# Attention in a recurrent-memory layer: scores turned keys-by-queries, row sums by a product with ones, division by exp(-ln(sum)), and filling work placed elsewhere

## The chip, the cores and the metric

The kernel runs on one core of one Trainium2 chip. The metric is the device time of one execution in microseconds (us). A run is one execution, and the medians below are of three or more runs. In the text PE is TensorE (the matrix engine), ACT is ScalarE, DVE is VectorE and POOL is GpSimd.

## The reference

The model alternates two kinds of layer, A, B, A, B, each on the normalized stream and each added back to it. Only layer B matters here. It is a recurrent-memory transformer: 2048 tokens in 64 segments of 32, width 640, 32 heads of 128, and 8 memory tokens that each segment hands to the next one.

```python
mask = (idx[:, None] < M) | (idx[:, None] >= idx[None, :])      # M = 8, L = 40
mem = mem0
for s in range(n_seg):                                          # 64, one after the other
    h = jnp.concatenate([mem, x[:, s*32:(s+1)*32, :]], axis=1)  # 40 tokens
    q, k, v = (jnp.einsum('btd,dhe->bhte', h, W) for W in (Wq, Wk, Wv))
    scores = jnp.einsum('bhqe,bhke->bhqk', q, k) * scale
    scores = jnp.where(mask[None, None], scores, -1000000000.0)
    p = _softmax(scores, axis=-1)
    o = jnp.einsum('bhqk,bhke->bhqe', p, v)
    o = jnp.einsum('bhte,hed->btd', o, Wo)
    mem = o[:, :M, :]                                           # needed by the next segment
    outs.append(o[:, M:, :])
```

(Shortened; layer A, a linear-memory attention with 32 heads of 20, is left out because nothing in it changes.)

## The kernel before

A segment is a *step*, and the two B layers have 128 steps in all. A step's memory rows come from the step before it, so steps follow each other. What doesn't depend on the memory is made ahead. The last 8 tokens of each segment, called tails, are projected for four segments at a time, one kind per step: V in steps with `i4 == 1`, Q in `i4 == 2`, K in `i4 == 3` (`i4` is the step's number modulo 4). In steps with `i4 == 0` the output product of the tail queries is made up for. This work is the *filling*: `fill(k)` puts some of it into PE's program where PE would otherwise wait. Layer normalization of a later group of tokens also belongs to the steps with `i4 == 2`, and its transposes to those with `i4 == 3`.

A wrapper in the program keeps each engine's instructions in the order in which the program issues them. The core of a step, where b is the half of the heads (16 of 32):

```python
def scores(b):
    sp = ps_tile([128, 8, 40], F32, "b_SP")
    nc.tensor.matmul(sp[:], lhsT=C.identb[:], rhs=mask[:]..., start=True, stop=False)   # adds the mask
    for h in range(16 * b, 16 * b + 16):                       # rows are queries: 64-column tiles, 2 at a time
        j, g, hh = b_slot_of_head(h)
        nc.tensor.matmul(sp[64*hh:64*hh+64, g % 8, :], lhsT=QT[s][:, 40*h:40*h+64], rhs=KT[s][:, 40*h:40*h+40],
                         start=False, stop=True, tile_position=(0, 64 * hh), ...)

def soft_1(b):
    nm = negmax[:, 8 * b:8 * b + 8]
    nc.vector.tensor_reduce(out=nm, in_=SP[b][:], axis=AX.X, op=ALU.max, negate=True)
    nc.vector.tensor_tensor(out=SP[b][:], in0=SP[b][:], in1=nm.unsqueeze(2)..., op=ALU.add)
    nc.scalar.activation(out=Pu[:, 8 * b:8 * b + 8, :], in_=SP[b][:], func=ACT.Exp)

def soft_2(b):
    nc.vector.tensor_reduce(out=ssum[:, 8*b:8*b+8], in_=Pu[:, 8*b:8*b+8, :], axis=AX.X, op=ALU.add)
    nc.vector.reciprocal(out=rs[:, 8*b:8*b+8], in_=ssum[:, 8*b:8*b+8])
    eng = nc.gpsimd if b == 0 else nc.vector
    ...                                                        # P = Pu * rs, two multiplications

def ptrans(b): ...                                             # 4 PE transposes of P: keys onto rows
```

```python
# ... Qa, Ka, Qb: thin products; their transposes TPQa, TPKa; Kb ...
scores(0)
TPQb = transp4(Qsb[:, 1, :], "b_TPQ");  scatter("act", TPQb, 1, heads(QT[s]), 0, 8, 24)
Va ...                                       # thin product for the first half of V
soft_1(0)
TPKb = transp4(Ksb[:, 1, :], "b_TPK");  scatter("dve", TPKb, 1, heads(KT[s]), 0, 8, 24)
Vb[:3] ...;  evac("act", Vsb[:, 0, :], Va[:])
scores(1);  soft_2(0);  soft_1(1)
Vb[3:] ...;  evac("act", Vsb[:, 1, :], Vb[:])
fill(5);  soft_2(1)
ptp = ptrans(0);  evac("dve", PTsb[:, 0], ptp);  fill(2)
ptp = ptrans(1);  ...;  fill(3)
...                                          # values: 64 products, 2 row tiles at a time, then evictions b_OTsb
fill(100)
op = OPass(lambda h: OTsb[:, h, 0:32], HORDER, "b_OPS");  op.run(100)      # output product
...                                          # layer norm of a later group in steps i4 == 2 (DVE, POOL)
nc.scalar.copy(msb[:], ops[:])
tps = [u.transposes() for u in units ...]    # tail transposes, between output product and memory product
...                                          # memory product b_MT, copies into hT of the next step
```

## Time and profile before

| | before |
|---|---|
| time, median of 4 runs | 3102.07 us (3101.28 to 3104.76) |
| steps with i4 = 0 / 1 / 2 / 3, start to start, median | 17.84 / 17.90 / 17.87 / 18.15 us |
| first B layer, first to last step's start | 1136.9 us |
| PE / DVE / ACT busy | 2744 / 1662 / 1326 us |

A step is timed here from the start of its first query product (b_Qa) to that of the next one. The two B layers together take about 2300 us of the 3100, so 0.1 us in a step is 12.8 us in the time.

From the page of the profile before: the span, the busy time of each engine with its share of the span, and two of the lines of 40 equal slices (digits are tenths: PE's busy share, and the granted TensorE clock).

```profile
span 3100.2 us, 118652 instructions
...
PE 2744.0 (89%) x52448; PEld 1465.0 (47%) x52448; DVE 1662.4 (54%) x4299; ACT 1326.2 (43%) x2799; POOL 606.1 (20%) x1819
...
PE   6888699999999999999778886999999999999997
...
PEclk9888799999999999999878897999999999999998
```

PE is at 9 in the slices of the B layers (the two long runs of nines), so PE's program bounds them. What little PE waits for there can be read in the list of waits of the profile before. Its columns are: what waited, for what, the total in us, how often, and the longest.

```profile
PE b_PTP L86 <- DVE b_P L86: 50.2, 98, 2.3
PE b_OPS L86 <- DVE b_OTsb L86: 44.3, 128, 0.4
PE b_MT L86 <- ACT b_msb L86: 35.1, 66, 0.5
PE b_Qa L86 <- DVE b_hT L86: 34.6, 126, 0.3
```

Together they come to 164 us, 1.3 us in each of the 128 steps. Here is where they sit, in the timeline of the profile before, in a step with K tails. The columns are start, duration, engine, line, operation, output and inputs; the bracket at the end gives the idle time before it and what ended it.

```profile
953.77 0.49 DVE L86 TENSOR_REDUCE b_ssum<-b_Pu 128x8 f32<-128x320 bf16 x1 [0.56 <-ACT b_Pu L86]
...
954.29 0.20 DVE L86 RECIPROCAL b_rs<-b_ssum 128x8 f32<-128x8 f32 x1
...
954.53 0.56 DVE L86 TENSOR_TENSOR b_P<-b_Pu,b_rs 128x256 bf16<-128x256 bf16 x2
...
955.01 0.42 PE L86 MATMUL b_PTP<-c_identb,b_P 128*128 128x128 bf16 x4 [0.37 <-DVE b_P L86]
...
957.39 2.36 PE L86 MATMUL b_OPS<-b_wo,b_OTsb 128*32 128x320 bf16 x64 [0.37 <-DVE b_OTsb L86]
...
959.68 0.62 PE L86 MATMUL b_ttp<-c_identb,b_tsb 128*128 128x128 bf16 x8
959.80 0.43 ACT L86 CAST b_msb<-b_OPS 128x320 bf16<-128x320 f32 x1 [2.21 <-PE b_OPS L86]
...
960.28 0.47 PE L86 MATMUL b_MT<-b_sel,b_msb 128*128 128x8 bf16 x6
```

DVE's chain of sum, reciprocal and multiplication ends just too late for the second transposes of the probabilities, and PE waits 0.37 us. After the output product, ACT needs 0.43 us to copy the result (b_msb) before the memory product may start. In this step the eight tail transposes (b_ttp, from 959.68 to 960.30) fill that time.

The view by windows gives the busy time in one step with i4 = 0 (first row) and one with i4 = 2 (second row), before:

```profile
core 0: us, PE busy (x) PEld busy (x) DVE busy (x) ACT busy (x) POOL busy (x), PEclk, DMA share, GB/s
889.25:907.09 17.84, 16.34 (x376) 9.22 (x376) 8.64 (x24) 6.82 (x18) 3.50 (x14) 1.00 0.06 13
924.99:942.87 17.88, 16.86 (x360) 9.04 (x360) 10.71 (x29) 6.84 (x18) 2.86 (x8) 1.00 0.06 14
```

PE is busy for 16.3 to 16.9 us of 17.9, DVE and ACT for less than 11. The clock is granted in full in both.

### The profile page before, as it was taken

How to read it: one execution, taken by the hardware profiler on the slowest of the kernel's cores; microseconds unless marked ns; L12 is line 12 of the kernel's file. 1: busy time of each engine (PE TensorE's matmuls, PEld its weight loads, DVE VectorE, ACT ScalarE, POOL GpSimd, SP SyncE). 2: the span in 40 equal slices, each digit the busy share in tenths (PEclk: the TensorE clock that was granted, in tenths of full speed). 3: DMA queues.
4: the chain of work that ended last, by engine and by line, in shares of the span. 5: the costliest groups of instructions: out<-in, count | busy, mean ns of one | idle time of the engine just before them, and what ended most of it. 6: DMA issues, size and time to landing. Idle time of an engine off the chain costs nothing. (4 is left out here: it accounts for less than half of the span.)

```text
span 3100.2 us, 118652 instructions
## 1 busy us (share of the span) xinstructions
PE 2744.0 (89%) x52448; PEld 1465.0 (47%) x52448; DVE 1662.4 (54%) x4299; ACT 1326.2 (43%) x2799; POOL 606.1 (20%) x1819
## 2 busy tenths in 40 slices
PE   6888699999999999999778886999999999999997
PEld 3444345554544555455434443454454545445553
DVE  4666355555555555555456663455555555555553
ACT  4666333334333434433256672333343443443432
POOL 2334211111111111111123441111111111111110
PEclk9888799999999999999878897999999999999998
DMA  7422300000000000000123333000000000000000
GB/s 259 131 92 88 117 14 17 18 20 18 18 18 17 17 19 19 17 16 16 33 76 111 111 99 113 13 15 17 16 15 17 15 15 16 18 15 16 14 12 11
DMA packets 98110, 131.53 MB, mean 42 GB/s; under 512 B 19872, under 2 KB 83376, under 8 KB 95664
## 3 DMA queue, kind: packets, MB, share of 16 engines
q1 hardware_dynamic: 95984, 122.19, 13.4%
q8 instruction: 412, 6.75, 0.9%
q10 hardware_dynamic: 1600, 1.66, 0.2%
q14 instruction: 114, 0.93, 0.1%
HBM read 89.17 MB, written 26.21 MB: 37 GB/s over the span
## 5 line engine op out<-in xcount | busy, mean ns | idle before, releaser
L86 PEld LDWEIGHTS <-b_hT 128*32 128x32 bf16 x15520 | 356.1, 96 | 376.6 <-DVE b_hT L86 46.5
L86 ACT ACTIVATE a_PT<-a_S 128x768 bf16<-128x768 f32 (+1 forms) x384 | 325.5, 891 | 83.7 <-PE a_S L86 73.7
L86 PE MATMUL b_OPS<-b_wo,b_OTsb 128*32 128x320 bf16 x8192 | 316.9, 309 | 44.3 <-DVE b_OTsb L86 44.3
L86 PE MATMUL b_V<-b_wv,b_hT 128*32 128x512 bf16 x5120 | 346.9, 382 | 0.0
L86 POOL TENSOR_TENSOR b_P<-b_Pu,b_rs 128x256 bf16<-128x256 bf16 (+1 forms) x256 | 111.6, 457 | 1180.5 <-DVE b_rs L86 1180.5
L86 PEld LDWEIGHTS <-b_OTsb 128*32 128x32 bf16 x8192 | 213.4, 99 | 117.3 <-DVE b_OTsb L86 58.0
L86 ACT ACTIVATE b_Pu<-b_SP 128x320 bf16<-128x320 f32 x256 | 112.0, 437 | 357.2 <-DVE b_SP L86 357.2
L86 ACT COPY b_QT<-b_TPQ 128x128 bf16<-128x128 bf16 x508 | 178.2, 379 | 119.7 <-PE b_TPQ L86 115.9
L86 DVE COPY b_KT<-b_TPK 128x128 bf16<-128x128 bf16 x382 | 101.7, 266 | 218.5 <-PE b_TPK L86 218.5
L86 DVE CAST b_hT<-b_MT 128x24 bf16<-128x24 f32 x126 | 23.0, 183 | 329.0 <-PE b_MT L86 329.0
L86 PE MATMUL b_Qa<-b_wq,b_hT 128*32 128x512 bf16 x2560 | 163.9, 385 | 34.6 <-DVE b_hT L86 34.6
L86 ACT CAST b_msb<-b_OPS 128x320 bf16<-128x320 f32 x128 | 54.5, 426 | 294.5 <-PE b_OPS L86 294.5
L86 DVE CAST b_Ksb<-b_Ka 128x512 bf16<-128x512 f32 x128 | 88.6, 692 | 150.1 <-PE b_Ka L86 150.1
L86 DVE TENSOR_REDUCE b_negmax<-b_SP 128x8 f32<-128x320 f32 x256 | 124.7, 487 | 71.1 <-PE b_SP L86 71.1
L86 DVE TENSOR_REDUCE b_ssum<-b_Pu 128x8 f32<-128x320 bf16 x256 | 123.1, 481 | 72.7 <-ACT b_Pu L86 72.7
L86 PE MATMUL b_Ka<-b_wk,b_hT 128*32 128x512 bf16 x2560 | 162.1, 382 | 0.0
L86 PE MATMUL b_Kb<-b_wk,b_hT 128*32 128x512 bf16 x2560 | 161.6, 381 | 0.0
L86 ACT ACTIVATE b_Qsb<-b_Qb 128x512 bf16<-128x512 f32 x128 | 76.4, 597 | 198.3 <-PE b_Qb L86 198.3
L86 PE MATMUL b_Qb<-b_wq,b_hT 128*32 128x512 bf16 x2560 | 160.8, 380 | 0.0
L86 PE MATMUL a_PP<-a_xnT,a_wt 128*128 128x512 bf16 x560 | 156.3, 415 | 2.1 <-DVE a_t1k L86 0.9
L86 DVE CAST b_Ksb<-b_Kb 128x512 bf16<-128x512 f32 x128 | 88.5, 692 | 125.8 <-PE b_Kb L86 125.8
L86 POOL TENSOR_SCALAR_AFFINE_SELECT a_PT<-a_PT 128x256 bf16<-128x256 bf16 x256 | 109.8, 433 | 213.5 <-ACT a_PT L86 200.4
(183 smaller groups left out, 5001.7 us busy)
## 6 DMA issues: line engine op xcount, KB each, us to landing
a_wt<-a_wpad SPq DMA_DIRECT2D x112, 160.0 KB
b_wo<-in_B_Wo_dram SPq DMA_DIRECT2D x8, 1280.0 KB
b_Vt<-b_Vtb SPq DMA_DIRECT2D x512, 16.0 KB
b_XO<-xres SPq DMA_DIRECT2D x256, 30.0 KB
a_wvo<-in_A_wo_dram SPq DMA_DIRECT2D x8, 800.0 KB
b_wq<-in_B_Wq_dram SPq DMA_DIRECT2D x5, 1024.0 KB
b_wk<-in_B_Wk_dram SPq DMA_DIRECT2D x5, 1024.0 KB
b_wv<-in_B_Wv_dram SPq DMA_DIRECT2D x5, 1024.0 KB
```

The lines of the kernel that those rows point to most:

```text
L86: r = f(*a, **k)
```

## The change

Its intent is to take work from PE and DVE. Scores are computed with keys on the rows, so the probabilities leave the exponential already in the layout that the value product reads, and no transposes of P are needed. The rows' maxima are dropped. The sums over keys are then sums over rows, and the change gives them to PE as a product with a matrix of ones, whose result has the sum on every row. Values are taken with the unnormalized probabilities, and each column of the result is divided by its sum afterwards, as multiplication by exp(-ln(sum)) with two ACT passes. Because exponentials without maxima could overflow, ACT's accumulator output adds up what it made. One test at the end of the kernel sees an overflow and runs a slower, general version if there was one. The filling is placed anew, budgeted in us.

```diff
-        pp = ctx.enter_context(tc.tile_pool(name="b_ps", bufs=8, space=PSUM))
+        pp = ctx.enter_context(tc.tile_pool(name="b_ps", bufs=4, space=PSUM))
+        pot = ctx.enter_context(tc.tile_pool(name="b_pot", bufs=2, space=PSUM))
 ...
             def scores(b):
-                for h in range(16 * b, 16 * b + 16):
-                    ...    # 64-column tiles, queries on rows
+                for r in range(4):
+                    for k, n in ((0, 32), (1, 8)):
+                        for j in range(4):
+                            h = 16 * b + 4 * j + r
+                            nc.tensor.matmul(sp[32*j:32*j+n, k, r, :], lhsT=KT[s][:, 40*h+32*k:40*h+32*k+n],
+                                             rhs=QT[s][:, 40*h:40*h+40], ..., tile_position=(0, 32 * j), ...)
+                acc = {} if general else {"accum_out": seen[:, b:b + 1]}
+                nc.scalar.activation(out=PT[:, b], in_=sp[:], func=ACT.Exp, **acc)
-            def soft_1(b): ...
-            def soft_2(b): ...
-            def ptrans(b): ...
+            def sums_and_values(b):
+                for jp in range(2):
+                    OTL[b, jp] = pot.tile([128, 2, 2, 256], F32, name="b_OTL", tag="ot")
+                ...                      # 8 products with ones (N = 160), then 32 value products, 4 row tiles at a time
+            def normalize(b, jp):
+                R = (wk if general else sm).tile([128, 2, 160], F32, name="b_R", tag="R")
+                o = OTL[b, jp]
+                nc.scalar.activation(out=R[:], in_=o[:, :, 1, 0:160], func=ACT.Ln)
+                acc = {} if general else {"accum_out": seen[:, 2 + 2 * b + jp:3 + 2 * b + jp]}
+                nc.scalar.activation(out=R[:], in_=R[:], func=ACT.Exp, scale=-1.0, **acc)
+                h = 16 * b + 8 * jp
+                nc.vector.tensor_tensor(out=OTsb[:, h:h + 8, :]..., in0=o[:, :, 0, 0:160], in1=R[:], op=ALU.mult)
 ...                                     # (the order of one step, after Qa, Ka, Qb and their transposes)
+            Va ...;  evac("act", Vsb[:, 0, :], Va[:])
+            scores(0)
+            Kb ...;  evac("dve", Ksb[:, 1, :], Kb[:])
+            while xn_pending:
+                ln_tr(xn_pending.pop(0))
+            TPQb ...;  scatter("act", TPQb, ...)
+            sums_and_values(0)
+            normalize(0, 0)
             TPKb = transp4(Ksb[:, 1, :], "b_TPK")
             scatter("dve", TPKb, 1, heads(KT[s]), 0, 8, 24)
 ...                                     # first 3 of 5 parts of Vb
             scores(1)
+            normalize(0, 1)
 ...                                     # last 2 parts of Vb
-            evac("act", Vsb[:, 1, :], Vb[:])
-            fill(5)
+            evac("dve", Vsb[:, 1, :], Vb[:])
+            fill(0.9)
+            sums_and_values(1)
+            normalize(1, 0)
+            normalize(1, 1)
             op = OPass(lambda h: OTsb[:, h, 0:32], HORDER, "b_OPS")
-            op.run(100)
+            op.run(8)
+            fill(0.7 if i4 else 0.9)
+            op.run(8)
+            fill(0.4)
+            ...                          # POOL adds seen to the running totals of the guard
 ...
-            tps = [u.transposes() for u in units if isinstance(u, TailUnit)]
 ...                                     # memory product, copies into hT
+                fill(9)
 ...
             for u in units:
                 if isinstance(u, TailUnit):
+                    u.transposes()
                     u.finish()
```

(Cut: the mask in its new layout, the general branch with its row maxima, the preloading of one ACT table at the start, and smaller things. "..." marks cuts inside lines too.)

## The prediction

> **What bounds the kernel now.** The two B layers run 64 steps each, one after the other. The start of the first query product recurs every 17.84 to 18.15 us (list of PE instructions in order of time), so B is about 128 x 17.94 = 2297 us of the 3101; the A layers, about 800 us, are untouched. Inside a step PE streams almost without a break at a granted clock near 1.0 (busy share 9 in every B slice; DVE and ACT 3 to 5). So PE's order bounds it: a step is about 15.8 us of PE work plus waits that the starts of matmuls show: about 0.45 us for the second probability transpose (behind VectorE's sum, reciprocal and scaling), 0.25 to 0.3 us for the value evictions, up to 0.6 us for the copy of the output before the memory product where nothing fills it, and 0.34 us for the new memory columns. Each change between column-tiled, row-tiled and whole-array products adds about 0.1 us (312 against 205 ns between starts). The Trainium skill, "TensorEngine Tiling (Array Packing)", Key Properties, says that changing the tiling mode drains TensorE; this agrees.
>
> **What the change does, per step.**
> - PE loses 8 transposes (0.66 us with their mode changes). It gains 32 more score products (four tiles at once; I expect no more than the 0.26 us per half seen now), 16 products with ones (estimate 0.14 us per half), and wider packing of values (from 11.4 towards 6 ns each). Filling moves behind the memory product and into the waits. Sum of PE work: estimate 15.6 us.
> - DVE loses two maxima, two subtractions, two sums, two reciprocals (about 3.3 us), one scaling (0.56) and the transposed copies (0.7); it gains four multiplications (0.5 each) for two evictions.
> - ACT gains eight passes of 320 columns (Ln, Exp), about 0.44 us each, and six accumulator outputs of unknown cost. Both functions lie in one table set (Trainium skill, "ScalarE: Activation LUTs", Table sets), so I expect a single table load at the start; the program shows one.
> - The critical point: ACT and DVE run in program order, and normalization stands before work that PE needs at once. First half: query scatters, Ln, Exp, multiplication, and only then the key scatter that the second scores need: PE waits about 0.6 us. Second half: Exp of scores, Ln, Exp, multiplication, then the eviction of V (0.69), then the values: about 2.5 us after the scores, against 1.3 us of PE work; PE waits about 1.2 us. Then the last multiplication against the output product (0.2 to 0.4), the copy before the memory product (0.25), and, in steps with Q or K tails, the last tail eviction before its transposes (0.6).
>
> So about 15.6 us of work plus 2.0 to 2.7 us of waits: what left PE comes back as waits on ACT and DVE. Laying both orders out with measured durations gives a step 0.2 us shorter (free accumulator outputs) to 0.4 us longer (0.12 us each).
>
> **Predicted:** 3105 us, 2990 to 3190 in 8 of 10. Faster by over 2%: 0.26; within 2%: 0.48; slower: 0.26.
>
> **What would show it.** DVE's busy time falls by about 300 us, ACT's rises by 250 to 400, PE's share falls to 80 to 85%. Waits: PE on the key scatter behind the multiplication, and on V's eviction in the second half. Steps with Q and K tails become the longest.
>
> **What would make it wrong.** Accumulator outputs dearer than 0.12 us (slower); Ln and Exp passes that overlap more, or less latency from PE to ACT than the 0.2 to 0.28 us read, five times in one chain (faster); small products not packing four wide (slower); the general branch being taken (far slower).

## More of the kernel before

The kernel before ran again beside each batch of experiments, with medians from 3101.07 to 3104.15 us, so times of different batches can be compared to about 3 us.

## The result, and the profile after

| | before | after |
|---|---|---|
| time, median of 4 runs | 3102.07 us | 3157.82 us (3157.01 to 3161.99) |
| ratio after/before | | 1.0181, 95% interval 1.0163 to 1.0199 |
| steps i4 = 0 / 1 / 2 / 3 | 17.84 / 17.90 / 17.87 / 18.15 | 17.77 / 17.77 / 19.07 / 19.46 us |
| first B layer, first to last step's start | 1136.9 us | 1166.5 us |
| PE / DVE / ACT busy | 2744 / 1662 / 1326 us | 2698 / 1359 / 1580 us |

Ratios are the mean time of one kernel's runs over the mean of the other's runs of the same rounds, so they are not quite the ratio of the medians quoted. The interval excludes no change at all: it is a loss of 1.8%. The first B layer lost 29.6 us and the second 31.5, together 61, which is all of the 60 us by which the two profiled spans differ. So everything happened in the steps, as it should have. The steps with i4 = 0 and 1 became slightly shorter. All the loss is in the steps with Q and K tails: 1.20 and 1.31 us each.

From the page of the profile after, the same lines:

```profile
span 3160.3 us, 128983 instructions
...
PE 2698.3 (85%) x57568; PEld 1443.2 (46%) x57568; DVE 1359.2 (43%) x3279; ACT 1580.0 (50%) x3953; POOL 530.0 (17%) x1569
...
PE   6888788888888888888778886888888888888887
...
PEclk9999799999999999999978996999999999999998
```

Less PE work (46 us) and much less DVE work (303 us), yet a longer time: PE's share fell to 85% (8 in place of 9 in the slices of the B layers), so it waits more. The granted clock is no lower than before. The page's chain of the work that ended last, after (shares of the span by engine, then by line), now has ACT and DVE links in it:

```profile
PE 48%; ACT 20%; DVE 16%; issue 6%; DMA 2%; POOL 1%; SPq 0%; DVEq 0%; ACTq 0%; POOLq 0%
ACT b_R L86 11%; DVE b_OTsb L86 6%; PE b_Qa L86 5%; PE b_V L86 5%; PE b_Kb L86 5%; PE b_Ka L86 4%; PE b_Qb L86 4%; PE b_SP L86 4%; PE b_OPS L86 3%; ACT b_QT L86 3%; DVE b_Vsb L86 2%; PE a_PP L86 2%; PE b_TPQ L86 2%; ACT b_PT L86 2%; PE b_OTL L86 2%
```

b_R is the pair of passes for exp(-ln(sum)), and b_OTsb is the multiplication by it. (The same chain of the profile before breaks off after 1% of the span, so it can't be compared.) PE's waits after:

```profile
PE b_OTL L86 <- DVE b_OTsb L86: 87.7, 128, 1.2
PE b_SP L86 <- DVE b_KT L86: 78.0, 128, 0.9
PE b_ttp L86 <- DVE b_tsb L86: 37.6, 64, 0.9
PE b_OTL L86 <- DVE b_Vsb L86: 36.3, 128, 0.3
...
PE b_OPS L86 <- DVE b_OTsb L86: 18.5, 93, 0.5
```

258 us in all, against 164. The first four are new, or nearly so (tail transposes waited for DVE's b_tsb for 3 us in all before). Of the old ones, that of the transposed P (50.2) is gone with its transposes, and those for hT (34.6) and msb (35.1) shrank to 2 and 3 us, because filling now stands before and behind the memory product. This list counts only time in which PE has nothing running by the profile's modelled ends; the gaps between starts, below, see more.

The timeline after shows how the first four arise (a step with Q tails; start, duration, engine and so on as above):

```profile
1170.00 0.46 ACT L86 ACTIVATE b_R<-b_OTL 128x320 f32<-128x320 f32 x1
...
1170.49 0.47 ACT L86 ACTIVATE b_R<-b_R 128x320 f32<-128x320 f32 x1
1170.87 0.19 ACT L86 ACTIVATION_READ_ACCUMULATOR b_R<-b_R 128x1 f32 x1
...
1171.14 0.49 DVE L86 TENSOR_TENSOR b_OTsb<-b_OTL,b_R 128x320 bf16<-128x320 f32 x1 [1.31 <-ACT b_R L86]
1171.55 0.48 DVE L86 COPY b_KT<-b_TPK 128x128 bf16<-128x128 bf16 x2
...
1171.82 0.38 PE L86 MATMUL b_SP<-b_QT,b_KT 128*32 128x40 bf16 x32 [0.54 <-DVE b_KT L86]
...
1172.31 0.44 ACT L86 ACTIVATE b_PT<-b_SP 128x320 bf16<-128x320 f32 x1 [1.25 <-PE b_SP L86]
...
1172.74 0.43 ACT L86 ACTIVATE b_R<-b_OTL 128x320 f32<-128x320 f32 x1
...
1173.20 0.47 ACT L86 ACTIVATE b_R<-b_R 128x320 f32<-128x320 f32 x1
...
1173.80 0.49 DVE L86 TENSOR_TENSOR b_OTsb<-b_OTL,b_R 128x320 bf16<-128x320 f32 x1 [1.76 <-ACT b_R L86]
1174.20 0.68 DVE L86 CAST b_Vsb<-b_V 128x512 bf16<-128x512 f32 x1
1174.34 0.31 PE L86 MATMUL b_OTL<-b_PT,b_ones 32*128 32x160 bf16 x6 [0.64 <-DVE b_OTsb L86]
...
1174.94 0.20 PE L86 MATMUL b_OTL<-b_PT,b_Vsb 32*128 32x40 bf16 x4 [0.28 <-DVE b_Vsb L86]
```

Read it from the top. DVE idles for 1.31 us until ACT has made the first inverse, multiplies, and only then copies the keys (b_KT) that PE has been waiting for. The transposes of those keys had started on PE at 1169.89 and been done long before. The Trainium skill, "Perfetto Trace Analysis", Per-engine timelines, says that DVE, ACT and GpSimd execute strictly first in, first out while only PE can pull weight loads ahead. The trace agrees as far as it goes: the key copy started 9.28 us into the step, behind the multiplication, and in run e1 below, which lets it go first, at 8.06. (This kernel's wrapper fixes the order as well, so no run here separates the two.)

In the second half ACT has three passes in a row, the exponential of the scores and the Ln and Exp of the second quarter of the heads, with an accumulator read after each exponential (in lines left out), and then comes DVE's multiplication. The second products with ones need one of only two PSUM tiles for their output, and the one they get is set free by the multiplication that ends this chain, at 1174.29. They wait 0.64 us. Then V's eviction, behind the same multiplication on DVE, holds up the values.

By windows, a step with i4 = 0 and one with i4 = 2, after:

```profile
1126.72:1144.49 17.77, 15.96 (x418) 9.10 (x417) 6.46 (x16) 8.26 (x25) 1.51 (x6) 1.00 0.06 14
1162.27:1181.34 19.07, 16.63 (x401) 8.90 (x401) 8.73 (x21) 9.45 (x28) 2.54 (x8) 1.00 0.06 13
```

In the first, PE's busy time fell by 0.38 us and the step by 0.07. In the second, PE's busy time fell by 0.23 and the step grew by 1.2. The starts of PE's instructions in such a step, worked out from the same trace, show the gaps one by one. A gap is the time from one start to the next; where the same pair exists without a wait, its length is set beside it:

| pair of PE starts, step i4 = 2, after | gap | same pair without a wait | lost |
|---|---|---|---|
| mask product to first score product, second half | 0.845 us | 0.240 (first half) | 0.60 |
| inside the products with ones, second half | 0.877 | 0.070 (first half) | 0.81 |
| products with ones to values, second half | 0.514 | 0.065 (first half) | 0.45 |
| inside the second half of the output product | 0.492 | 0.136 (its first half) | 0.36 |
| filling to memory product | 0.480 | 0.312 (same pair in run e10 below) | 0.17 |
| inside the tail transposes | 0.903 | 0.056 (the others of the group) | 0.85 |

In the steps with i4 = 0 and 1 the first five are there too, nearly the same (only the gap in the output product is shorter with i4 = 0, 0.365 us), and the last isn't. In K-tail steps the first gap is 1.20 us and the last 0.690.

The last Q-tail and the last K-tail step of each B layer are a control within this trace, because no group of tokens is left to be normalized. In that Q-tail step the gap in the tail transposes is 0.690 us in place of 0.903, and the step takes 18.85 us. In that K-tail step the first gap is 0.79 us in place of 1.20, and the step takes 18.80. So the longer tail wait of the Q-tail steps goes with the layer normalization, and the longer wait for the keys in the K-tail steps with the transposes of its result and what follows from them. The tail transposes themselves (eight, 0.42 us of PE starts) also count in full now. Before, they stood where PE was waiting for b_msb anyway.

### The profile page after: what moved, and what is told of

The parts are those of the page before. It is cut to its first block, busy times and chain, and to the rows that moved or that the text cites. A ratio compares the mean times of both kernels' runs of the same rounds, so it can differ in the third digit from the quotient of the medians.

```text
span 3160.3 us, 128983 instructions
## 1 busy us (share of the span) xinstructions
PE 2698.3 (85%) x57568; PEld 1443.2 (46%) x57568; DVE 1359.2 (43%) x3279; ACT 1580.0 (50%) x3953; POOL 530.0 (17%) x1569
## 4 chain that ended last, share of the span: by engine, by line
PE 48%; ACT 20%; DVE 16%; issue 6%; DMA 2%; POOL 1%; SPq 0%; DVEq 0%; ACTq 0%; POOLq 0%
ACT b_R L86 11%; DVE b_OTsb L86 6%; PE b_Qa L86 5%; PE b_V L86 5%; PE b_Kb L86 5%; PE b_Ka L86 4%; PE b_Qb L86 4%; PE b_SP L86 4%; PE b_OPS L86 3%; ACT b_QT L86 3%; DVE b_Vsb L86 2%; PE a_PP L86 2%; PE b_TPQ L86 2%; ACT b_PT L86 2%; PE b_OTL L86 2%
## 5 line engine op out<-in xcount | busy, mean ns | idle before, releaser
L86 DVE TENSOR_TENSOR b_OTsb<-b_OTL,b_R 128x320 bf16<-128x320 f32 x512 | 251.8, 492 | 669.5 <-ACT b_R L86 669.5
L86 PEld LDWEIGHTS <-b_hT 128*32 128x32 bf16 x15520 | 393.7, 96 | 318.4 <-issue 29.3
L86 PE MATMUL b_OPS<-b_wo,b_OTsb 128*32 128x320 bf16 x8192 | 357.5, 308 | 20.5 <-DVE b_OTsb L86 18.5
L86 POOL TENSOR_TENSOR c_tot<-c_tot,b_seen 128x2 f32<-128x2 f32 (+1 forms) x256 | 50.5, 197 | 1871.4 <-ACT b_PT L86 1306.1
L86 ACT ACTIVATE b_R<-b_OTL 128x320 f32<-128x320 f32 x512 | 223.7, 437 | 211.0 <-PE b_OTL L86 211.0
L86 ACT ACTIVATE b_R<-b_R 128x320 f32<-128x320 f32 x512 | 241.5, 472 | 16.3
L86 ACT ACTIVATE b_PT<-b_SP 128x320 bf16<-128x320 f32 x256 | 112.2, 438 | 161.5 <-PE b_SP L86 158.6
L86 PE MATMUL b_OTL<-b_PT,b_ones 32*128 32x160 bf16 (+1 forms) x2048 | 111.8, 235 | 89.5 <-DVE b_OTsb L86 87.7
L86 ACT ACTIVATE b_Qsb<-b_Qa 128x512 bf16<-128x512 f32 x128 | 76.6, 598 | 177.6 <-PE b_Qa L86 175.8
L86 PE MATMUL b_SP<-b_QT,b_KT 128*32 128x40 bf16 (+1 forms) x8192 | 96.9, 181 | 78.0 <-DVE b_KT L86 78.0
```

The source lines that it names most:

```text
L86: r = f(*a, **k)
```

## The experiments

The theory, from the prediction and the traces: **order**. What left PE came back as waits, because on ACT and DVE, which work in program order, the new normalization was issued ahead of work that PE needs sooner. Rival 1: **PE itself pays**, for the many small products and the mode changes of the tiled array (the skill, "TensorEngine Tiling (Array Packing)", Key Properties, says that switching the tiling mode drains TensorE; here the step from column-tiled products to whole-array ones took 312 ns between starts against 205 ns without a change). Rival 2: **the new operations are too dear**, above all the accumulator outputs, in any order.

All kernels gave correct results. "Steps" are the medians for i4 = 0 / 1 / 2 / 3; in e3 the K-tail steps fall into two groups, and the median hides one of them.

| run | made from | median us | ratio to before | 95% | steps, us |
|---|---|---|---|---|---|
| e1_key_first | after | 3067.71 | 0.9883 | 0.9867 to 0.9900 | 17.16 / 17.16 / 18.47 / 18.49 |
| e2_v_first | after | 3094.57 | 0.9974 | 0.9958 to 0.9991 | 17.29 / 17.29 / 18.59 / 18.98 |
| e3_tail_early | after | 3198.33 | 1.0305 | 1.0288 to 1.0323 | 17.76 / 17.76 / 20.51 / 18.77 |
| e4_no_accum | after | 3096.72 | 0.9977 | 0.9960 to 0.9994 | 17.30 / 17.30 / 18.61 / 18.99 |
| e5_order4 | after | 2963.85 | 0.9556 | 0.9541 to 0.9572 | 16.70 / 16.70 / 17.10 / 17.34 |
| e6_tail_ln | after | 3114.82 | 1.0038 | 1.0022 to 1.0055 | 17.75 / 17.75 / 18.10 / 18.76 |
| e7_before_no_max | before | 3041.85 | 0.9805 | 0.9788 to 0.9821 | 17.37 / 17.90 / 17.41 / 17.69 |
| e8_triple_sums | after | 3156.31 | 1.0178 | 1.0161 to 1.0195 | 17.75 / 17.75 / 19.05 / 19.44 |
| e9_inv_early | after | 2980.99 | 0.9608 | 0.9592 to 0.9624 | 16.39 / 16.43 / 17.74 / 18.12 |
| e10_order5 | e5 | 2881.55 | 0.9289 | 0.9273 to 0.9304 | 15.97 / 15.97 / 16.38 / 17.03 |
| e11_order5_no_accum | e10 | 2836.61 | 0.9142 | 0.9126 to 0.9157 | 15.61 / 15.65 / 16.06 / 16.66 |
| e12_order5_pool_guard | e10 | 2852.86 | 0.9196 | 0.9180 to 0.9211 | 15.68 / 15.71 / 16.11 / 16.72 |

### e1_key_first: the key copy before the first multiplication

Normalization is split into `inverse` (Ln and Exp on ACT) and `normalize` (the multiplication on DVE), and DVE's order of two instructions is swapped. No work is added or removed.

```diff
                 sums_and_values(0)
-                normalize(0, 0)
+                inverse(0, 0)
             TPKb = transp4(Ksb[:, 1, :], "b_TPK")
             scatter("dve", TPKb, 1, heads(KT[s]), 0, 8, 24)
+            if not general:
+                normalize(0, 0)
```

> The changed kernel with one move on VectorE: the copy of the second half's keys goes before the multiplication that ends the first normalization; no work is added or taken away. Order theory (PE waits because ScalarE and VectorE run in program order): in the changed kernel the second scores start 842 ns (1201 ns in the steps with a norm transpose) after their mask product, where the first scores start 240 ns after theirs; that excess of 0.60 (0.96) us goes, mean 0.69 us a step, 128 steps, about 88 us: about 3070 us. Rival (the loss lies in the work itself, in the halved pool of PSUM buffers or in the small products, and a wait taken away here only turns up at the next one): 3135 us or more.

Measured: 3067.71 us, 90 us less than after, or 0.70 us per step. Swapping two instructions of one engine turned the loss into a gain of 1.2%. The steps show that it is this one gap and nothing else. The gap between the mask product and the second scores fell to 0.240 us, the length that it has in the first half; it had been 0.84 us, and 1.20 in the K-tail steps. So 0.60 us should be saved in three kinds of step and 0.96 in those with K tails, and the steps fell by 0.61, 0.61, 0.60 and 0.97. With that, the K-tail steps are as long as the Q-tail steps (18.49 and 18.47 us). Two other differences between them remain and happen to cancel: the transposes of the normalized group take 0.24 us of PE's program in the K-tail steps, and their tail transposes wait 0.21 us less (0.690 against 0.90).

### e2_v_first: V's eviction before the second multiplication

```diff
             scores(1)
-            normalize(0, 1)
+            inverse(0, 1)
             ...
             evac("dve", Vsb[:, 1, :], Vb[:])
+            normalize(0, 1)
```

> The changed kernel with one other move on VectorE: the eviction of V's second half goes before the second multiplication of the first half. Order theory: the 514 ns between the last product with ones and the first value product fall to the 65 ns of the first half, 0.45 us a step, about 58 us: about 3100 us. Rival (work, PSUM buffers): 3140 us or more.

Measured: 3094.57 us, 63 us less than after, or 0.48 us in each kind of step. The gap between the products with ones and the values fell from 514 to 3 ns, since V is there by then. The gap inside the products with ones stayed (872 ns): they still wait for the multiplication. So this order takes away one of the two waits of the second half, and e9 finds a better one.

### e3_tail_early: the whole tail product before the memory product

```diff
             ops = op.ps
-            fill(0.4)
+            fill(9 if i4 >= 2 else 0.4)
```

The tails' last eviction then runs while PE makes the memory product, so the tail transposes shouldn't wait.

> The changed kernel with the last tail product of the steps with Q and K tails put before the memory product instead of behind it, so that its eviction comes before the tail transposes need it. Those steps are 1.3 and 1.7 us longer than the others now, and inside their transposes stand gaps of 0.90 and 0.69 us. Order theory: 0.6 to 0.8 us less in half of the steps, about 0.35 us a step, 40 to 50 us: about 3112 us. Rival: the wait is the new memory columns' and moves there, 3145 us or more.

This expectation failed. The time rose by 40 us to 3198.33. The usual K-tail step did fall by 0.69 us, as expected, and so did the last Q-tail step of each layer, in which nothing is normalized (18.85 to 18.17 us). But the 28 Q-tail steps with a normalization rose by 1.44 us, and 12 of the 30 K-tail steps took 20.0 to 21.7 us. The timeline of this run in such a step (DVE and PE, as above):

```profile
1193.88 0.69 DVE L86 TENSOR_SCALAR b_tsb<-b_tail 128x512 bf16<-128x512 f32 x1 [1.48 <-PE b_tail L86]
...
1194.49 0.88 DVE L86 BATCH_NORM_STATS2 b_ln_st<-b_xt 128x6 f32<-128x320 bf16 x2
...
1196.46 0.49 DVE L86 TENSOR_SCALAR b_xt<-b_xt,b_ln_mv,b_ln_rstd 128x640 bf16<-128x640 bf16 x1 [0.67 <-POOL b_ln_rstd L86]
...
1196.87 0.17 DVE L86 CAST b_hT<-b_MT 128x24 bf16<-128x24 f32 x1
...
1197.30 1.04 PE L86 MATMUL b_Qa<-b_wq,b_hT 128*32 128x512 bf16 x8 [2.28 <-ACT b_hT L86]
```

DVE waits idle for the tail product, evicts it (b_tsb), then makes the whole layer normalization of a later group, with a detour over POOL, and only then copies the new memory columns (b_hT; ACT copies the rest of them just after), for which PE waits 2.28 us. In the kernel after, DVE had done that normalization while PE was still busy. It is the same mechanism, one engine's order, in a place that I had overlooked: moving PE's filling shifted DVE's program against PE's.

The 12 long K-tail steps each follow such a wait. By windows (columns as above), a long one and a usual one:

```profile
1197.30:1217.35 20.05, 17.88 (x406) 9.42 (x405) 6.87 (x16) 10.01 (x29) 1.86 (x7) 0.93 0.08 21
1273.38:1292.15 18.77, 16.60 (x406) 9.10 (x405) 6.87 (x16) 10.00 (x29) 1.86 (x7) 1.00 0.09 22
```

Both have the same instructions, but the granted clock is 0.93 in the first and 1.00 in the second. In the 12 long steps it was 0.86 to 0.93 and in the other 18 it was 1.00, and the 12 are together about 22 us longer than the usual step would make them. In e6 below, in which the wait is gone, no K-tail step has a lowered clock, so the lost clock goes with the wait. Why it followed only 12 of the 28 waits is not shown.

### e4_no_accum: no accumulator outputs

The guard is taken away, so this kernel isn't safe for other inputs; it only measures. The six `accum_out` arguments and POOL's two additions go.

> The changed kernel without the accumulator outputs of its exponentials (so without the guard that these feed in layer B; the result on these inputs stays right). The trace shows a read of the accumulator of 188 to 196 ns after each, of which about 0.09 us is not hidden. If they stand in the chain that PE waits for, five of the six count: 0.45 us a step, about 58 us: about 3100 us. If they are hidden: 3150 us or more.

Measured: 3096.72 us, 61 us less than after, 0.48 us per step or 0.08 per accumulator output. That is about the whole loss. So rival 2 has a share: with the order as it was, free accumulator outputs would have made the change even with the kernel before. But it isn't the whole answer, as e5, e9 and e10 show with all six outputs in place.

### e5_order4: all four moves together

e1, e2 and e3, and the layer normalization moved to a stretch in which DVE is idle anyway (its transposes stay one step later):

```diff
+            g_need = (s + 6) // 4                     # right after the key copies of the first half
+            if s % 4 == 2 and g_need < NT:
+                ln_norm(g_need)
+                ln_fresh.append(g_need)
             Va, vparts = thin_parts(vcols, W.wv, 0, "b_V")
             ...
-            g_need = (s + 6) // 4                     # from behind the output product
-            if s % 4 == 2 and g_need < NT:
-                ln_norm(g_need)
-                xn_pending.append(g_need)
             ...
+            xn_pending, ln_fresh = xn_pending + ln_fresh, []      # at the end of the step
```

> The changed kernel with four moves in program order and the same work: keys before the first multiplication, V's eviction before the second, the last tail product before the memory product, and the layer norm of the next token group moved from the end of the step (in front of the copy of the new memory columns) to VectorE's idle stretch before the second keys' eviction. Order theory: the gains add up: 90 us (keys) and 63 us (V) as measured alone, about 48 us for the tails once the norm is out of their way: 3158 - 201, about 2957 us, between 2935 and 2990. If the waits only change places: above 3030 us.

Measured: 2963.85 us, 4.4% under before, with the same instructions as in the change. e1, e2 and e6 save 90 + 63 + 43 = 196 us one at a time, and together they save 194: these three waits add up.

### e6_tail_ln: e3 and the moved normalization, without e1 and e2

```diff
+            if s % 4 == 2 and g_need < NT:            # right after the key copies of the first half, as in e5
+                ln_norm(g_need)
+                ln_fresh.append(g_need)
             ...
-            fill(0.4)
+            fill(9 if i4 >= 2 else 0.4)
             ...
-            if s % 4 == 2 and g_need < NT:            # from behind the output product, as in e5
-                ln_norm(g_need)
-                xn_pending.append(g_need)
```

> The changed kernel with the last tail product before the memory product (the move that lost 40 us alone) and the layer norm moved to VectorE's idle stretch. Theory: that move lost because in the steps with a norm VectorE then waited for the tail product, ran the whole norm after it and only then copied the new memory columns (2.5 us between the tail transposes and the next query product); with the norm away, these steps fall from 20.5 us to about 18.3, those with K tails stay at 18.77: about 3110 us. If the move is bad in itself: 3180 us or more.

Measured: 3114.82 us. Against e3, where only the place of the normalization differs, it is 83.5 us faster, most of it in the 28 Q-tail steps with a normalization, which fell by 2.41 us (20.51 to 18.10 us, 67 us in all). The rest is in the K-tail steps: none of them has a lowered clock or takes over 18.8 us any more. This confirms the reading of e3. The Q-tail and K-tail steps are now 0.97 and 0.70 us shorter than in the kernel after, and the others haven't moved.

### e7_before_no_max: one part of the change alone, on the kernel before

```diff
             def soft_1(b):
-                nm = negmax[:, 8 * b:8 * b + 8]
-                nc.vector.tensor_reduce(out=nm, in_=SP[b][:], axis=AX.X, op=ALU.max, negate=True)
-                nc.vector.tensor_tensor(out=SP[b][:], in0=SP[b][:], in1=nm.unsqueeze(2)..., op=ALU.add)
                 nc.scalar.activation(out=Pu[:, 8 * b:8 * b + 8, :], in_=SP[b][:], func=ACT.Exp)
```

Again a kernel without a guard, to measure only.

> The kernel before without its row maxima and their subtraction, nothing else changed (right on these inputs, no guard). This takes 4 VectorE passes of about 0.5 us a step. VectorE is not the bound, but one pair of them stands in the chain from the second scores to the second probability transpose, for which PE waits 0.44 us in three steps of four (b_P before b_PTP: 103 us of waits before weight loads). Chain theory: that wait goes, and nothing else: 40 to 55 us less, about 3055 us. If off-path VectorE work costs nothing at all: 3100 us; if VectorE's load bound the step: 4 x 0.49 x 128, some 250 us less.

Measured: 3041.85 us, 2.0% under before; the interval touches the 2% line, so whether it is over 2% is unclear. The steps of three kinds fell by 0.46 to 0.47 us, the size of the old wait before the second transposes of P, and in this run's trace that wait is gone (311 ns between the starts in a Q-tail step, against 755 before). The steps with i4 = 1 didn't change, because they never had it: their gap was 312 ns in the kernel before already. That makes about 45 of the 60 us. The rest is in the first and last steps of the two layers (the last whole ones before took 19.3 to 20.0 us at a granted clock of 0.83 to 0.91, and now 16.7 at 1.00). So dropping the maxima alone pays. With the rest of the change and its order, the same kernel loses 116 us again.

### e8_triple_sums: PE's new small products done three times in the second half

```diff
-                for k, n in ((0, 32), (1, 8)):
+                for k, n in (1, 3)[b] * ((0, 32), (1, 8)):
```

The repeats start the same sums anew, so the result doesn't change.

> The changed kernel with the products with ones of the second half done three times over (the same values written again; the result is right). That adds 16 products, about 0.3 us of PE work a step. Order theory: in that half PE waits another 0.5 us for V's eviction after these products anyway, so they are free: the time of the changed kernel, 3158 us, within 6. Rival (the small row-tiled products are what the change paid with): 0.3 x 128, about 38 us more, 3196 us.

Measured: 3156.31 us, against 3157.82. Sixteen more products per step cost nothing, because PE waits right there for V's eviction: with eight products they and the gap behind them took 0.96 + 0.51 = 1.47 us, with 24 of them 1.25 + 0.22 = 1.47 us. Rival 1 falls for this place: PE's small products aren't what the time is spent on. Elsewhere it wasn't tested in this way, but e10 below does the same PE work in a common step of 15.97 us, in place of 17.77.

### e9_inv_early: Ln and Exp of the second quarter before the exponential of the second scores

```diff
+            if not general:
+                inverse(0, 1)
             scores(1)
             normalize(0, 1)
```

Only ACT's order changes. ACT had been idle for 1.25 us before that exponential (bracket at 1172.31 in the timeline after), and the sums of the second quarter had long been there.

> The changed kernel with one move on ScalarE: Ln and Exp for the second quarter of the heads go before the second scores instead of behind their exponential; they need nothing from these scores. Order theory: the multiplication then ends near 10.3 us in the step instead of 12.0, and V's eviction near 11.1 instead of 12.6, while PE comes to the second products with ones at 11.2: both waits there (0.87 us inside the products with ones, 0.45 us before the values) go, about 1.3 us a step, 170 us: about 2990 us. This one move would turn the change from slower to faster than the kernel before (3102). Rival (the exponential of the second scores, now behind them, holds PE as long): 3120 us or more.

Measured: 2980.99 us, 177 us less than after (1.38 us per step) and 3.9% under before, by moving two instructions. In its trace the gap inside the second products with ones is 70 ns, that before the values 65 ns, as in the first half: the lines "b_OTL <- b_OTsb" (87.7 us) and "b_OTL <- b_Vsb" (36.3 us) are gone from PE's waits, while the one for b_KT (77.3 us) and that for b_tsb (37.6 us) stand as they were. This was the largest single item.

### e10_order5: e5 with e9's order

```diff
+            if not general:
+                inverse(0, 1)
             scores(1)
-            inverse(0, 1)
+            normalize(0, 1)
             ...
             evac("dve", Vsb[:, 1, :], Vb[:])
-            normalize(0, 1)
```

> The four moves together (2964 us) and this fifth one, with the second multiplication back in front of V's eviction. Left in the four-move kernel are 0.87 us a step before the second products with ones; of that all but about 0.1 us should go: about 0.8 x 128 = 102 us less, 2862 us, between 2845 and 2885. If the waits only pass on to the last multiplication and the output product: above 2920 us.

Measured: 2881.55 us, 7.1% under before and 8.7% under after, with every operation of the change still in it. It is inside the range that was expected but 20 us above its middle. The parts no longer add up: e1, e6 and e9 save 90 + 43 + 177 = 310 us singly, and here 276. The traces show where most of the other 34 went: with the keys earlier, PE comes sooner to the second half and waits for V's eviction again. The gap between the products with ones and the values is 0.20 to 0.24 us (0.51 in the K-tail steps), against 0.06 in e9, 27 us more over all steps. The K-tail steps are still 1.06 us longer than those with i4 = 0. In the last one of each layer, without transposes of a normalized group, it is only 0.41, as in the Q-tail steps (16.38 against 15.97 us). So 0.65 us go with these transposes: 0.24 in PE's program and 0.41 in the longer wait for V's eviction.

### e11_order5_no_accum and e12_order5_pool_guard: the price of the guard

e11 is e10 without accumulator outputs and thus without a guard. e12 keeps a guard: the two outputs at the exponentials of the scores stay, and the inverses are added up by POOL into a running tile, from which the same final test reads. POOL was busy for only 17% of the span in the kernel after. The edit of e11 (and of e4):

```diff
-                acc = {} if general else {"accum_out": seen[:, b:b + 1]}                          # scores
+                acc = {}
...
-                acc = {} if general else {"accum_out": seen[:, 2 + 2 * b + jp:3 + 2 * b + jp]}    # normalize
+                acc = {}
...
-            if not general:
-                nc.gpsimd.tensor_tensor(out=C.tot[:, 0, 0:2], in0=C.tot[:, 0, 0:2], in1=seen[:, 0:2], op=ALU.add)
-                nc.gpsimd.tensor_tensor(out=C.tot[:, 1, 0:4], in0=C.tot[:, 1, 0:4], in1=seen[:, 2:6], op=ALU.add)
```

and the core of that of e12, which also lets the final test read the new tile:

```diff
-                acc = {} if general else {"accum_out": seen[:, 2 + 2 * b + jp:3 + 2 * b + jp]}
-                nc.scalar.activation(out=R[:], in_=R[:], func=ACT.Exp, scale=-1.0, **acc)
+                nc.scalar.activation(out=R[:], in_=R[:], func=ACT.Exp, scale=-1.0)
+                if not general:
+                    for c0, n in ((0, 128), (128, 128), (256, 64)):
+                        nc.gpsimd.tensor_tensor(out=C.totR[:, 0:n], in0=C.totR[:, 0:n],
+                                                in1=R[:].rearrange("p j c -> p (j c)")[:, c0:c0 + n], op=ALU.add)
```

> The five moves without the accumulator outputs, so without the guard in layer B: what the guard still costs there. Of the six reads, the two before the last multiplication and, if ScalarE is again what PE waits for, that of the second exponential stand in the chain, 0.09 us each: 0.2 to 0.3 us a step, 25 to 40 us less than with them.

Measured: 2836.61 us, 45 us less than e10, a little more than the 25 to 40 expected.

> The five moves with the guard kept, but fed otherwise: the four accumulator outputs of the inverses go, and GpSimd, busy 17% of the time in the changed kernel, adds the inverses themselves into a running tile (three additions of up to 128 columns for each inverse, about 1.2 us, 4.8 us a step, estimated from its 362 ns for 84 columns). The two reads after the exponentials of the scores stay. If GpSimd's work stays off the chain: most of the 45 us that leaving out all six reads gave, 30 to 40 us less than 2882: about 2847 us. If GpSimd now holds up the buffers of the inverses or its copies for the next step: 2890 us or more.

Measured: 2852.86 us. This is the fastest version that keeps a guard, 8.0% under before and 9.7% under after. POOL's busy time doubled (530 to 1086 us), and still the time is only 16 us above that of e11, which has no guard. (No run gave either guard inputs that overflow, so that they catch one is not shown.)

The accumulator's price can be read directly. ACT in e10, two Ln/Exp pairs in a row:

```profile
1084.81 0.47 ACT L86 ACTIVATE b_R<-b_R 128x320 f32<-128x320 f32 x1
1085.19 0.19 ACT L86 ACTIVATION_READ_ACCUMULATOR b_R<-b_R 128x1 f32 x1
1085.28 0.42 ACT L86 ACTIVATE b_R<-b_OTL 128x320 f32<-128x320 f32 x1
```

and the same place in e11:

```profile
1084.86 0.47 ACT L86 ACTIVATE b_R<-b_R 128x320 f32<-128x320 f32 x1
1085.24 0.42 ACT L86 ACTIVATE b_R<-b_OTL 128x320 f32<-128x320 f32 x1
```

From start to start it is 0.47 us with the read and 0.38 without: the read's record lasts 0.19 us, and it costs 0.09. The second figure also agrees with the skill, "ScalarE: Activation LUTs", What ACT_TABLE_LOAD costs, which says that ACTIVATEs in a row overlap by about 93 ns: here an instruction of 0.47 us was followed after 0.38.

### What couldn't be tried or wasn't run

A version that divides on DVE, in place of Ln, Exp and a multiplication, doesn't build: both of its inputs would be in PSUM, and the build refuses that. A version with DVE's reciprocal of the sums built but wasn't run. From the groups of the profile before (count, busy us, mean ns of one), the reciprocal's time goes with the columns:

```profile
L86 DVE RECIPROCAL b_rs<-b_ssum 128x8 f32<-128x8 f32 x256 | 51.9, 203 | 8.9
L86 DVE RECIPROCAL a_i<-a_r 128x32 f32<-128x32 f32 x48 | 16.9, 353 | 2.1 <-DVE a_r L86 0.3
```

(353 - 203) / 24 is 6.25 ns per column, so 320 columns would take an estimated 2.15 us, against 0.91 us for Ln and Exp (437 and 472 ns). That speaks for the way over ACT, though no run compares the two: once the sum stands on every row there are 320 columns to invert instead of 8.

## Why the prediction was right

Its mechanism held, point by point.

- **PE's work falls, and the gain comes back as waits.** PE's busy time fell by 46 us, and PE's waits in the list rose from 164 to 258 us. e1, e2 and e9 change nothing but the order of instructions on ACT and DVE, and each wins back more than the 56 us lost, by closing the gaps that the table names. So it is shown, not only argued, that the gain went into waits that the order made.
- **The waits, term by term.** Keys behind the multiplication: 0.6 us predicted, 0.60 measured. Second half: 1.2 predicted, 0.81 + 0.45 = 1.26 measured. Output product: 0.2 to 0.4 predicted, 0.36 measured. The copy before the memory product: 0.25 predicted, 0.17 measured. Tail eviction: 0.6 predicted, 0.85 in Q-tail steps and 0.63 in K-tail steps (0.690 less 0.056) measured.
- **The small products pack four wide.** 32 score products start within 0.20 us, 6.4 ns each, against 16.4 ns each before; values went from 11.4 to 6.4 ns; 8 products with ones took about 0.15 us as estimated. The Trainium skill, "TensorE: Matmul & The Clock Gate", Wait — 56ns, not 53.3ns?, says that starts never come closer than about 25 ns however small the product. For one tile position that agrees: four products, one on each tile, start every 25 ns in the traces (a new group of four at 1169.52, .55, .57, .60).
- **The busy times.** DVE fell by 303 us (300 predicted), ACT rose by 254 (250 to 400 predicted), PE's share is 85% (80 to 85 predicted). One table load, of 1.3 us, stands in the trace after (as in that before), as the skill's "ScalarE: Activation LUTs", Table sets, let one expect of functions that share a set.
- **The longest steps** are those with Q and K tails, as predicted.

What was off is the size, by 53 us: 3105 predicted, 3157.82 measured, inside the range of 2990 to 3190. The net effect was forecast as next to nothing (3 us, with faster and slower equally likely) and came out as a loss of 56. Per step that is 0.44 us, just outside the 0.2 shorter to 0.4 longer of the layout. That "within 2%" came true at 1.8% is in part luck. Two terms were mis-sized.

- *"Six accumulator outputs of unknown cost"* were taken at less than half of their range: on the prediction's own scale (a step 0.2 us shorter with free outputs, 0.4 longer at 0.12 us each), 3105 us corresponds to about 0.045 us each. They cost 0.09 (0.47 against 0.38 us from start to start), which on the same scale is about 0.22 us more per step, an estimated 28 of the 53 us. Removing all six was worth 0.48 us per step.
- *The steps with tails* were taken as the common step plus one wait of 0.6 us. In fact the move of the tail transposes behind the memory product cost twice: they wait 0.63 to 0.85 us for their eviction, and their own 0.42 us, which used to fill the wait for b_msb, now count in full. In the K-tail steps the wait for the keys is 0.96 us in place of 0.60 as well; the transposes of the normalized group and ACT's copy of them stand ahead of the query copies there, and in the one K-tail step of each layer without them the wait is 0.55 us (0.79 less 0.24). So these two kinds of step took 19.07 and 19.46 us, where 15.6 + 2.7 = 18.3 was the most that the prediction's sum gave. The other two kinds, at 17.77, are within it.

I made one mistake of the same kind later: e3's expectation counted what PE would save and not what DVE does in between.

What stays open: whether the halving of the PSUM pool (8 to 4 buffers) costs anything (no wait for it shows in the trace after, and no run tested it alone). A few steps take up to 3 us longer than the others of their kind. In the trace after they are the first and the last ones of each layer, at a granted clock of 0.78 to 0.91, where the other steps have 1.00. How much of their extra time the clock accounts for was not worked out.

## What to carry to other kernels

Work taken from the bounding engine is a gain only if what replaces it isn't issued ahead of something that the bounding engine needs sooner: before such a change, write down for each engine in program order what PE waits for next, and issue ready work for PE (a copy of keys, an inverse whose sum is there) before work that is itself still waiting. When the time doesn't follow the busy time, compare gaps between starts on PE with the same pair elsewhere in the step where it doesn't wait; each gap names the instruction to move, and here three moves without any change in work were worth 63 to 177 us each. Judge a change in its best order and not only in the order in which it was handed over: this one is 1.8% slower as it stood and 7.1% faster after reordering alone (8.0% with the guard's sums moved to POOL as well).

## What the Trainium skill lacked or had wrong

- "ScalarE: Activation LUTs", What it computes, says that an ACTIVATE can give an accumulator output, but no page gives its price. It shows as an instruction of its own (ACTIVATION_READ_ACCUMULATOR, 188 to 196 ns), of which 0.09 us add to the time until ACT's next instruction (0.47 against 0.38 us from start to start). Six per step were worth 61 us in the change's order and 45 us in the best order.
- The same page, What ACT_TABLE_LOAD costs, gives 186 ns + 0.833 ns per column with immediate scale and bias, an estimated 453 ns for 320 columns, and doesn't tell apart the memory that is read. Here, at 320 columns, Ln from PSUM took 437 ns, Exp from PSUM 438 and Exp from SBUF 472. So it wasn't the function, and reading SBUF in place of PSUM went with 34 ns more (these Exps also write back to the tile that they read, which no run separates).
- "TensorEngine Tiling (Array Packing)", Key Properties, says that a change of tiling mode drains TensorE, but gives no time. Here a change from column-tiled to whole-array products cost about 0.1 us (312 ns between starts against 205 without a change).
- "VectorE: DVE Perf Modes", First, the fixed hardware budget, says that Reciprocal repeats its iterative divide, but gives no time per element. It was 203 ns for 8 columns and 353 for 32, 6.25 ns per column. With it one sees at once that a reciprocal of sums kept in 8 columns is cheap and one of 320 columns is not.
